# Another order for the attention row: scores, then attention products, then the transposes of both heads

## The chip, the cores and the metric

The kernel runs on one core of a Trainium2 chip. The metric is the device time of one execution in microseconds (us). Before the change three runs took 401.72, 405.03 and 405.11 us, median 405.03 us.

## The reference: what is computed

Inputs are q, k and v (4 batches, 8 heads, 768 positions, 64 numbers per head). For each block of 32 keys a summary key (the maximum over the block) and a summary value (the mean) are made. Each query sees the keys less than 16 positions away and all 24 summaries:

```
scores_l = scale * q @ k^T            (masked to |i - j| < 16)
scores_s = scale * q @ k_sum^T + log(32)
a        = softmax(concat(scores_l, scores_s))
x        = a @ concat(v, v_sum)       -> heads side by side: 4 x 768 x 512
h        = relu(x @ w_in)             -> 4 x 768 x 1024
gate     = sigmoid(conv of h over 3 positions)
out      = (h * gate) @ w_out         -> 4 x 768 x 512
```

All of it is float32. The two large products are made from float32r parts, three products each (high x high, high x low, low x high).

## The kernel before

**Tiling.** The sequence of each batch is cut into two halves, which gives 8 chunks of 384 positions (`NCHUNK`). In each chunk the 8 heads are taken as 4 pairs. A pair is one *row* of attention work; there are 32 rows. The first product of a chunk (x @ w_in, `f1`, line 404) is cut into 8 *units* of 128 hidden features; a unit is 12 matmuls into one PSUM bank. The second product (`f2`, line 473) is cut into tiles of 128 positions; its matmuls are dealt out over the units, 6, 9 or 12 of them after each first product.

**A row.** A row has three sorts of matmul on TensorE (PE in the profile): the scores of a pair (`qk`, line 260, tile `pq`, 24 passes), the transposes of the softmax of each head (`tr`, line 308, tile `pt`, three per head) and the attention products (`av`, line 329, tile `xp`, 24 passes). They belong to different pairs: in the step with number j the scores are those of pair j/2, the transposes those of the pair before, the attention products those of the pair before that. Around them, VectorE (DVE) subtracts the maximum (line 278), ScalarE (ACT) does six exponentials (288) and a small sum (296), VectorE the reciprocal (297), GpSimd (POOL) scales (300). ACT copies a transposed head out of PSUM (315, `aT`). The attention product leaves PSUM as a high part (ACT, 349, `xh`) and a low part (DVE, 350, `xl`), and these are the input of the first product of the next chunk.

**The gate chain of a unit.** After `f1`: relu (ACT 422), middle tap (ACT 425, or DVE 427 in chunks 3, 5, 6 and 7), two taps (DVE 434), tanh (ACT 451), gate multiply (DVE 452, the last reader of the unit's PSUM bank), high part `ghi` (ACT 455), low part `glo` (POOL 456). `gates(1)` issues the multiply of a unit two units later.

**What sets the order.** In chunks 0 and 1 a scheduler orders all engines. From chunk 2 on (`ORDERED`) PE runs in the order in which `unit` writes it, and only the other engines are ordered by the scheduler. A step j falls in unit u of chunk c by j = 8(c+1) + 3 + u, so even steps, which hold the row, fall in odd units. In such a unit the order on PE is: transposes of the first head, attention products, scores, transposes of the second head, first product, second product. Odd steps (even units) hold loads, and for the rows of an even chunk one small transpose `pv` (line 234), which turns the summary values; its result `vm` is copied by ACT (236).

**PSUM.** There are eight banks: two for `pq` (tag s), one for all `pt` (tag t), one that `xp` and `pv` share (tag x), three for the first product (tag f1), one for the second (tag f2). Buffers of a tag are dealt out in turn, and a matmul that takes a buffer waits until the last reader of its former owner is done.

Of the kernel before, what the change touches and what calls it, by code (L numbers as in the profile page):

```python
# [7 lines left out]
F32 = mybir.dt.float32  # L8
# [8 lines left out]
P = 128  # L17
# [8 lines left out]
NP = H // 2  # L26
# [19 lines left out]
ORDERED = 2  # L46
# [4 lines left out]
def attention_ffn(ctx, tc, qT, kT, vT, v4, w_in, cwT, w_out, mask8, ident_in, out):  # L51
# [3 lines left out]
    ps = ctx.enter_context(tc.tile_pool(name="ps", bufs=1, space=bass.MemoryType.PSUM))  # L55
# [19 lines left out]
    def warm(where, after=None):  # L75
        def go():
            for i in range(WARM.get(where, 0)):
                nc.tensor.matmul(pw, idle[:, :P], idle, start=True, stop=True)  # L78

        if after is None:  # L80
            go()
        else:
            with tc.issue_after(after):
                go()
# [28 lines left out]
    def split_in(fc, t):  # L113
        weights(t, flat(win_hi, fc), flat(win_lo, fc), f"i{fc}")
# [6 lines left out]
    def split_out(fc, t):  # L121
        weights(t, wout_hi[:, fc, :], wout_lo[:, fc, :], f"o{fc}")
# [14 lines left out]
    for tag in ("xh", "xl"):  # L137
        t = sp.tile([P, 2, KL], F32, tag=tag, name=f"k_{tag}", bufs=2)
        spare += [t[:, 0, :], t[:, 1, :]]

    def ins(x):
        return getattr(x, "ins", x)
# [7 lines left out]
    def load_k(c, p):  # L150
        b, hf = divmod(c, 2)
        i = c * NP + p
        st = state[(c, p)] = {}
        if i == NP - 1:
            kw = sp.tile([P, 1024], F32, tag="stage", name=f"kw{i}", bufs=2)
            st["kw"] = kw[:, : CB * NK].rearrange("p (b k) -> p b k", b=CB)
        else:
            st["kw"] = sp.tile([P, CB, NK], F32, tag="kw", name=f"kw{i}", bufs=3)
        if hf == 0:
            if c == 0:  # L160
                k = spare[p]
            else:
                k = sp.tile([P, KL], F32, tag="kT", name=f"kT{i}", bufs=2)
            nc.sync.dma_start(k, kT[b, p, :, :KL])
            st["k"] = k
        if c:
            first = kT[b, p, :, hf * CH : hf * CH + WK]
            nc.sync.dma_start(st["kw"][:, :, :WK], window(first, 1, [SP, P], WK))

    def load_vt(c, p):  # L170
        b, hf = divmod(c, 2)
        i = c * NP + p
        if hf:
            return
        if b == 0:
            v = raw_b[:, 2 + p, :S].bitcast(F32)
        else:
            v = sp.tile([P, 1024], F32, tag="stage", name=f"vt{i}", bufs=2)[:, :S]
        nc.sync.dma_start(v, vT[b, p])
        state[(c, p)]["vt"] = v  # L180

    def load_q(c, p):
        b, hf = divmod(c, 2)
        q = sp.tile([P, CH], F32, tag="q", name=f"q{c}_{p}", bufs=4)
        nc.sync.dma_start(q, qT[b, p, :, hf * CH : (hf + 1) * CH])
        state[(c, p)]["q"] = q

    def load_v(c, p):
        b, hf = divmod(c, 2)
        i = c * NP + p  # L190
        va = sp.tile([P, CB, P], F32, tag="va", name=f"va{i}", bufs=4)
        first = v4[b, p, hf * CH : hf * CH + WK, :]
        nc.sync.dma_start(va[:WK, :, :], window(first, P, [P, WK], P))
        state[(c, p)]["va"] = va

    def load_vm(c, p):
        vm = state[("vm", c // 2, p)]
        nc.sync.dma_start(
            state[(c, p)]["va"][WK:NK, :, :], vm.unsqueeze(1).to_broadcast([NB, CB, P])
        )  # L200
# [20 lines left out]
    def vmean_pair(c, p):  # L221

        b, hf = divmod(c, 2)
        if hf:
            return
        st = state[(c, p)]
        vs = sp.tile([P, NB], F32, tag="vs", name=f"vs{c}_{p}", bufs=2)
        nc.vector.tensor_reduce(
            vs, st["vt"].rearrange("p (n t) -> p n t", t=BLK), AX.X, ALU.add
        )  # L230
        pv = ps.tile(
            [P, 512], F32, tag="x" if c else "f1", name=f"pv{c}_{p}", bufs=1 if c else 3
        )
        nc.tensor.transpose(pv[:NB, :P], vs, ident)  # L234
        vm = cp.tile([NB, P], F32, tag=f"vm{p}", name=f"vm{c}_{p}")
        nc.scalar.activation(vm, pv[:NB, :P], AF.Copy, scale=1.0 / BLK)
        if c == 0:
            nc.gpsimd.tensor_copy(
                st["va"][WK:NK, :, :], vm.unsqueeze(1).to_broadcast([NB, CB, P])
            )  # L240
        state[("vm", b, p)] = vm
# [6 lines left out]
    def qk(c, p):  # L248


        st = state[(c, p)]
        n = c * NP + p
        pq = [
            ps.tile([P, 512], F32, tag="s", name=f"pq{n}_{h}", bufs=2) for h in range(2)
        ]
        for blk in range(CB):
            i, half = divmod(blk, 2)
            for h in range(2):
                r = slice(h * QB, (h + 1) * QB)
                last = nc.tensor.matmul(  # L260
                    pq[h][half * QB : (half + 1) * QB, i * NK : (i + 1) * NK],
                    st["q"][r, blk * QB : (blk + 1) * QB],
                    st["kw"][r, blk, :],
                    start=True,
                    stop=True,
                )
        if c == 0:
            warm(f"pq{p}", ins(last))
        softmax(n, c % 2, pq)
# [33 lines left out]

    def tr(j):
        a = state.pop(("a", j))
        pt = ps.tile([P, 512], F32, tag="t", name=f"pt{j}")
        for i in range(3):
            last = nc.tensor.transpose(pt[:NK, i * P : (i + 1) * P], a[:, i, :], ident)  # L308
        if j < 2 * NP:
            warm("tr", ins(last))  # L310
        aT = sp.tile([P, 3 * P], F32, tag="aT", name=f"aT{j}", bufs=3)
        if j < 2 * NP and j % 2:
            nc.vector.tensor_copy(aT[:NK, :], pt[:NK, : 3 * P])
        else:
            nc.scalar.copy(aT[:NK, :], pt[:NK, : 3 * P])  # L315
        state[("aT", j)] = aT
# [42 lines left out]
    def slot(j):  # L359

        if j % 2 == 0:
            n = j // 2 + 2
            if NP <= n < npair:
                load_k(*divmod(n, NP))
                load_vt(*divmod(n, NP))
            if NP <= j // 2 < npair:
                load_vm(*divmod(j // 2, NP))
            if j // 2 < npair:
                qk(*divmod(j // 2, NP))
        else:  # L370
            n = (j + 1) // 2
            if NP <= n + 1 < npair:
                load_q(*divmod(n + 1, NP))
            if n < npair:
                c, p = divmod(n, NP)
                if c:
                    vmean_pair(c, p)
                    load_v(c, p)
                prep_pair(c, p)

    def slot_t(j):
        if 0 <= j - DEPTH < NGROUP:
            tr(j - DEPTH)

    def slot_av(j):
        n = j - DEPTH - 2
        if n % 2 == 0 and 0 <= n < NGROUP:
            av(n // 2)
# [166 lines left out]
    def rooms():  # L555
        gated["hi"] = cp.tile([P, NFC, S], F32R, name="ghi", tag="big_a")
        gated["lo"] = cp.tile([P, NFC, S], F32R, name="glo", tag="big_b")
# [12 lines left out]
    def unit(c, u, pieces, together):  # L570


        j = 8 * (c + 1) + 1 + DEPTH + u
        last = c == NCHUNK - 1
        if together and j % 2 == 0:


            slot_t(j)
            slot_av(j)
        slot(j)  # L580
        if together and j % 2 == 0:
            slot_t(j + 1)
        elif together and c == ORDERED and u == 0:
            slot_t(j)
        if c == 0 and u < 2:
            for fc in (4 + 2 * u, 5 + 2 * u):
                split_in(fc, raws[fc])
        if c == 0 and u == 2:
            rooms()
        gates(1)  # L590
        early = c == 0 and u < EARLY_IN
        if not early:
            f1(c, u, [0, 1])
        if not together:
            slot_t(j)
        done = f1(c, u, [3] if early else [2, 3])
        if c == 0:
            warm("unit", ins(done))
        gate_conv(c, u)
        pending.append((c, u))  # L600
        assert len(pending) <= 2
        if not together:
            slot_av(j)
        for x in pieces[u]:
            f2(*x)
        if last:
            gates(0)
        at = NFC * c + u
        for fc in range(NFC):
            if OUT_AT[fc] == at:  # L610
                split_out(fc, raws["o", fc])
        for fc in range(NFC):
            if OUT_AT[fc] == at + 1:
                raws["o", fc] = load_out(fc)
# [71 lines left out]
```

## Time and profile before

| what | value |
|---|---|
| three runs | 401.72, 405.03, 405.11 us |
| profiled execution | 405.19 us, span 403.3 us |
| PE busy | 387.8 us (96%) |
| DVE, ACT, POOL busy | 262.9, 255.8, 150.3 us |
| chain that ended last | PE 85%, ACT 5%, DVE 3%, DMA 3%, POOL 2% |
| mean granted TensorE clock | 0.987 |

The 1.9 us between the profiled execution and its span lie around the span. A timeline row gives the start of an instruction, its length, engine, line, result and operands; matmuls overlap, so the time that one takes from the next is read from start to start. Chunks 0 and 1 end at about 130 us; the rows that the change touches stand from 134 to 330 us.

### The profile page before, as it was taken

Reading aid. Unit: us, or ns where it says so; the run is one execution under the profiler, and the core shown is the slowest. Engines: PE = TensorE matmul, PEld = TensorE weight load, DVE = VectorE, ACT = ScalarE, POOL = GpSimd, SP = SyncE. Lnnn points to the kernel's source line nnn. Section 1 sums busy time; section 2 is a strip of 40 time slices with the busy share of each in tenths; the row PEclk is TensorE's granted clock in tenths of the full one; section 3 lists DMA queues with packets and bytes.
Section 4 is the critical chain, followed back from the end, with each engine's and each line's share of the span. In section 5 each row is a group of like instructions: output and inputs, shape, how many; then the busy total and the mean of one; then the engine's idle time right before and its main releaser. Section 6 shows DMA issues by size and latency. Waiting matters only on the chain.

```text
span 403.3 us, 8835 instructions
## 1 busy us (share of the span) xinstructions
PE 387.8 (96%) x3173; PEld 322.2 (80%) x3173; DVE 262.9 (65%) x777; ACT 255.8 (63%) x806; POOL 150.3 (37%) x179
## 2 busy tenths in 40 slices
PE   8989879999989999999999999999999999999996
PEld 3546558787768888888888888888888888999884
DVE  4889969998976665667765466466565655556200
ACT  3575699998876787766666778666666653343211
POOL 2316565377764234332333333332422242222200
PEclk9999799999899999999999999999999999999999
DMA  8999783666896784546233343334220000000011
GB/s 293 337 367 191 203 212 119 210 199 194 237 205 188 229 261 127 150 148 199 68 101 112 79 114 113 101 98 120 67 63 28 28 2 26 26 28 27 28 52 52
DMA packets 60715, 54.47 MB, mean 135 GB/s; under 512 B 24640, under 2 KB 51328, under 8 KB 60672
## 3 DMA queue, kind: packets, MB, share of 16 engines
q1 hardware_dynamic: 56928, 47.19, 41.2%
q10 hardware_dynamic: 3744, 6.73, 4.5%
q8 instruction: 25, 0.41, 0.5%
q14 instruction: 18, 0.15, 0.1%
HBM read 45.55 MB, written 6.29 MB: 129 GB/s over the span
## 4 chain that ended last, share of the span: by engine, by line
PE 85%; ACT 5%; DVE 3%; DMA 3%; POOL 2%; issue 1%; SPq 0%; DVEq 0%; POOLq 0%
PE f L473 33%; PE f L404 32%; PE pq L260 7%; PE xp L329 5%; PE pt L308 5%; PE pw L78 3%; ACT a L288 2%; DMA va<-v 2%; DMA k_xh<-kT 1%; POOL wout_lo L128 1%; DVE a L300 1%; POOL glo L456 0%; ACT wu_o L97 0%; ACT t L425 0%; PE pv L234 0%
## 5 line engine op out<-in xcount | busy, mean ns | idle before, releaser
L456 POOL TENSOR_TENSOR glo<-t,ghi 128x383 fp32r<-128x383 f32 (+1 forms) x64 | 66.3, 1037 | 138.3 <-ACT ghi L455 125.9
L404 PE MATMUL f<-xh,win_hi 128*128 128x384 f32 (+1 forms) x256 | 92.5, 361 | 0.9 <-ACT win_hi L127 0.9
L434 DVE SCALAR_TENSOR_TENSOR t<-f,cw,t 128x382 f32<-128x382 f32 (+3 forms) x128 | 78.8, 615 | 19.2 <-ACT t L425 16.6
L404 PE MATMUL f<-xl,win_hi 128*128 128x384 f32 (+1 forms) x256 | 87.9, 344 | 0.0
L404 PE MATMUL f<-xh,win_lo 128*128 128x384 f32 (+1 forms) x256 | 87.2, 341 | 0.0
L288 ACT ACTIVATE a<-a,nm 128x120 f32<-128x120 f32 x192 | 73.4, 384 | 12.3 <-DVE nm L278 12.1
L473 PE MATMUL f<-wout_lo,ghi 128*128 128x512 f32 x192 | 75.7, 394 | 1.6 <-POOL wout_lo L128 1.6
L473 PE MATMUL f<-wout_hi,ghi 128*128 128x512 f32 x192 | 76.4, 398 | 0.0
L473 PE MATMUL f<-wout_hi,glo 128*128 128x512 f32 x192 | 75.0, 391 | 0.0
L300 POOL TENSOR_TENSOR a<-a,sm 128x360 f32<-128x360 f32 x56 | 45.7, 837 | 45.6 <-ACT f L422 28.1
L451 ACT ACTIVATE t<-t 128x383 f32<-128x383 f32 (+1 forms) x64 | 33.6, 526 | 40.3 <-DVE t L434 39.6
L452 DVE SCALAR_TENSOR_TENSOR t<-t,f 128x383 f32<-128x383 f32 (+1 forms) x64 | 35.2, 552 | 29.6 <-ACT t L451 29.6
L404 PEld LDWEIGHTS f<-xh,win_hi 128*128 128x128 f32 x256 | 49.3, 192 | 5.1 <-ACT win_hi L127 1.2
L404 PEld LDWEIGHTS f<-xl,win_hi 128*128 128x128 f32 x256 | 49.2, 192 | 1.4 <-issue 0.3
L404 PEld LDWEIGHTS f<-xh,win_lo 128*128 128x128 f32 x256 | 48.9, 191 | 0.2
L278 DVE CUSTOM_DVE_ANT_0 a<-pq,mask 128x120 f32<-128x120 f32 x192 | 42.7, 275 | 1.5 <-PE pq L260 1.3
L473 PEld LDWEIGHTS f<-wout_lo,ghi 128*128 128x128 f32 x192 | 36.1, 188 | 7.9 <-POOL wout_lo L128 2.2
L473 PEld LDWEIGHTS f<-wout_hi,glo 128*128 128x128 f32 x192 | 36.1, 188 | 7.7
L473 PEld LDWEIGHTS f<-wout_hi,ghi 128*128 128x128 f32 x192 | 36.2, 188 | 7.0 <-issue 0.5
L315 ACT COPY aT<-pt 120x384 f32<-120x384 f32 x60 | 28.2, 470 | 20.7 <-PE pt L308 20.7
L422 ACT ACTIVATE f<-f 128x384 f32<-128x384 f32 (+1 forms) x64 | 30.4, 475 | 15.8 <-PE f L404 15.6
L308 PE MATMUL pt<-ident,a 128*120 128x128 f32 x192 | 33.7, 283 | 5.1 <-ACT aT L315 3.1
(59 smaller groups left out, 508.8 us busy)
## 6 DMA issues: line engine op xcount, KB each, us to landing
va<-v SPq DMA_DIRECT2D x32, 288.0 KB, 4.2
kw<-kT SPq DMA_DIRECT2D x28, 288.0 KB, 6.4
q<-qT SPq DMA_DIRECT2D x32, 192.0 KB, 4.5
out_dram<-ob ACTq DMA_DIRECT2D x24, 256.0 KB, 2.0
kT<-kT SPq DMA_DIRECT2D x12, 392.0 KB, 3.9
vt<-vT SPq DMA_DIRECT2D x12, 384.0 KB, 4.3
wo<-w_out SPq DMA_DIRECT2D x8, 512.0 KB, 5.3
raw_a<-w_in SPq DMA_DIRECT2D x6, 512.0 KB, 11.5
```

What stands on the lines that cost most here:

```text
L260: last = nc.tensor.matmul(pq[h][half * QB : (half + 1) * QB, i * NK : (i + 1) * NK], st["q"][r, blk * QB : (blk + 1) * QB], st["kw"][r, bl ...
L278: nc.vector.tensor_tensor_reduce(a[:, i, :], pq[h][:, i * NK : (i + 1) * NK], mask[:, hf, i, :], -0.125, 3.0e38, ALU.add, ALU.min, nm[:, h ...
L288: nc.scalar.activation(a[:, i, :], a[:, i, :], AF.Exp, bias=nm[:, h, i : i + 1], scale=-1.0, accum_out=sm[:, h, i : i + 1],)
L300: (nc.gpsimd if n >= NP else nc.vector).tensor_tensor(a, a, sm[:, h, :].unsqueeze(2).to_broadcast([P, 3, NK]), ALU.mult)
L308: last = nc.tensor.transpose(pt[:NK, i * P : (i + 1) * P], a[:, i, :], ident)
L404: last = nc.tensor.matmul(ph[:, :n], w[:, fc, cc, :], x[:, cc, :n], start=(cc == 0 and m == 0), stop=(cc == NCC - 1 and m == 2),)
L422: nc.scalar.activation(h[:, :n], h[:, :n], AF.Relu)
L434: nc.vector.scalar_tensor_tensor(t[:, i0:i1], h[:, hf + k - 1 + i0 : hf + k - 1 + i1], cw[:, fc, k : k + 1], t[:, i0:i1], ALU.mult, ALU.add,)
L451: nc.scalar.activation(t, t, AF.Tanh, scale=0.5)
L452: nc.vector.scalar_tensor_tensor(t, t, 1.0, h[:, hf : hf + ng], ALU.add, ALU.mult)
L456: nc.gpsimd.tensor_tensor(gated["lo"][:, fc, d0 : d0 + ng], t, hi.bitcast(F32), ALU.subtract)
L473: nc.tensor.matmul(po, gx[:, fc, ss], w[:, fc, :], start=(fc == 0 and m == 0), stop=(fc == NFC - 1 and m == 2),)
```

## The change

From chunk 2 on the row is written in another order: scores, attention products, transposes of the first head, transposes of the second head, then the first product as before. The transposes of the second head no longer use the bank of tag t but take a buffer of the three of tag f1.

```
     def tr(j):
         a = state.pop(("a", j))
-        pt = ps.tile([P, 512], F32, tag="t", name=f"pt{j}")
+
+        own = j % 2 == 0 or j <= 2 * NP * (ORDERED + 1) + 1
+        pt = ps.tile(
+            [P, 512], F32, tag="t" if own else "f1", name=f"pt{j}", bufs=1 if own else 3
+        )
...
         j = 8 * (c + 1) + 1 + DEPTH + u
         last = c == NCHUNK - 1
         if together and j % 2 == 0:
-
-
+            slot(j)
+            slot_av(j)
             slot_t(j)
-            slot_av(j)
-        slot(j)
-        if together and j % 2 == 0:
             slot_t(j + 1)
-        elif together and c == ORDERED and u == 0:
-            slot_t(j)
+        else:
+            slot(j)
+            if together and c == ORDERED and u == 0:
+                slot_t(j)
```

There are 18 such rows (units 1, 3, 5, 7 of chunks 2 to 5, units 1 and 3 of chunk 6), and in unit 5 of chunk 6 a row without scores. The lines behind `tr` stand 4 lines further down in the changed kernel (308 becomes 312, 422 becomes 426, and so on).

The order on PE in unit 5 of chunk 4 before (pt: transposed head, xp: attention products, pq: scores, f_4_5: first product of the unit):

```order
L308 MATMUL pt_3206<-ident,a_0_3106 120x128 x3
L329 MATMUL xp_3212<-aT_3066,va_2888 64x64
...
L260 MATMUL pq_0_3234<-kw_2948,q_0_3026 64x120
...
L308 MATMUL pt_3268<-ident,a_1_3113 120x128 x3
L404 MATMUL f_4_5_3278<-xh_2393,win_hi 128x384
```

and now:

```order
L260 MATMUL pq_0_3213<-kw_2923,q_0_3026 64x120
...
L333 MATMUL xp_3247<-aT_3122,va_2888 64x64
...
L312 MATMUL pt_3262<-ident,a_0_3085 120x128 x3
L312 MATMUL pt_3268<-ident,a_1_3092 120x128 x3
L408 MATMUL f_4_5_3278<-xh_2424,win_hi 128x384
```

The scores come first and the six transposes stand together ahead of the first product.

The order on ACT from the relu of unit 2 to the relu of unit 3 in chunk 4 before (f_4_2, f_4_3: first products, by relu; t_1, t_2: gate tiles, by tap and tanh; a_0, a_1: the exponentials of the row's two heads; ob: a finished tile of the output):

```order
L422 ACTIVATE f_4_2_3035<-f_4_2_3035 128x384
L455 CAST ghi<-t_1_3013 128x383
L425 ACTIVATE t_2_3049<-f_4_2_3035,cw 128x383
L482 ACTIVATE ob_2_3059<-f_1_2_2913 128x512
L315 COPY aT_3066<-pt_3062 120x384
L483 DMA out_dram<-ob_2_3059 128x512
L349 CAST xh_2942<-xp_3068 128x384
L451 ACTIVATE t_2_3049<-t_2_3049 128x383
L315 COPY aT_3128<-pt_3124 120x384
L288 ACTIVATE a_0_3106,sm_3105<-a_0_3106,nm_3104 128x120 x3
L288 ACTIVATE a_1_3113,sm_3105<-a_1_3113,nm_3104 128x120 x3
L422 ACTIVATE f_4_3_3134<-f_4_3_3134 128x384
```

and now:

```order
L459 CAST ghi<-t_1_3013 128x383
L426 ACTIVATE f_4_2_3035<-f_4_2_3035 128x384
L429 ACTIVATE t_2_3049<-f_4_2_3035,cw 128x383
...
L455 ACTIVATE t_2_3049<-t_2_3049 128x383
L288 ACTIVATE a_0_3085,sm_3084<-a_0_3085,nm_3083 128x120 x3
L288 ACTIVATE a_1_3092,sm_3084<-a_1_3092,nm_3083 128x120 x3
L353 CAST xh_2977<-xp_3103 128x384
L296 ACTIVATE sm_3084<-sm_3084 128x6
L319 COPY aT_3122<-pt_3118 120x384
L319 COPY aT_3128<-pt_3124 120x384
L426 ACTIVATE f_4_3_3134<-f_4_3_3134 128x384
```

The high part `xh` and both copies `aT` have moved from ahead of the exponentials to behind them, ahead of the relu of unit 3; and the cast of unit 1 now stands ahead of the relu of unit 2.

The order on DVE around the row of unit 5 of chunk 4 before (t_4: gate tile of unit 4; nm, a: the maximum step of the row):

```order
L452 SCALAR_TENSOR_TENSOR t_4_3193<-t_4_3193,f_4_4_3179 128x383
L350 TENSOR_TENSOR xl_2943<-xp_3212,xh_2942 128x384
L278 ISA a_0_3250,nm_3248<-pq_0_3234,mask 128x120
...
L278 ISA nm_3248 128x1
L297 RECIPROCAL sm_3249<-sm_3249 128x6
```

and now:

```order
L456 SCALAR_TENSOR_TENSOR t_4_3193<-t_4_3193,f_4_4_3179 128x383
L278 ISA a_0_3229,nm_3227<-pq_0_3213,mask 128x120
...
L278 ISA nm_3227 128x1
L354 TENSOR_TENSOR xl_2978<-xp_3247,xh_2977 128x384
L297 RECIPROCAL sm_3228<-sm_3228 128x6
```

The low part `xl` has moved behind the six maximum steps.

## Rows read from the trace of the kernel before

**Rows 1.** Windows: stretch, length, busy us (instructions) by engine, granted clock, DMA share, GB/s.

```profile
130.00:173.00 43.00, 43.00 (x387) 37.95 (x387) 27.62 (x87) 32.20 (x102) 14.91 (x20) 1.00 0.65 195
```

**Rows 2.** Page, part 4: the chain that ended last, by engine.

```profile
PE 85%; ACT 5%; DVE 3%; DMA 3%; POOL 2%; issue 1%; SPq 0%; DVEq 0%; POOLq 0%
```

**Rows 3.** Timeline, PE, the row in unit 3 of chunk 4.

```profile
230.60 0.39 PE L473 MATMUL f<-wout_hi,glo 128*128 128x512 f32 x1
230.83 0.49 PE L308 MATMUL pt<-ident,a 128*120 128x128 f32 x3
231.25 0.92 PE L329 MATMUL xp<-aT,va 120*64 120x64 f32 x24
232.10 0.84 PE L260 MATMUL pq<-kw,q 64*64 64x120 f32 x24
232.88 0.55 PE L308 MATMUL pt<-ident,a 128*120 128x128 f32 x3
233.18 0.42 PE L404 MATMUL f<-xh,win_hi 128*128 128x384 f32 x1
```

**Rows 4.** Timeline, PE, other neighbours of these matmuls: chunk 1, and the row without scores.

```profile
82.53 0.49 PE L308 MATMUL pt<-ident,a 128*120 128x128 f32 x3
82.77 0.42 PE L404 MATMUL f<-xh,win_hi 128*128 128x386 f32 x1
...
107.25 0.40 PE L473 MATMUL f<-wout_lo,ghi 128*128 128x512 f32 x1
107.49 0.39 PE L473 MATMUL f<-wout_hi,glo 128*128 128x512 f32 x1
107.81 0.62 PE L260 MATMUL pq<-kw,q 64*64 64x120 f32 x6
108.36 0.45 PE L329 MATMUL xp<-aT,va 120*64 120x64 f32 x6
...
328.63 0.92 PE L329 MATMUL xp<-aT,va 120*64 120x64 f32 x24
329.48 0.54 PE L308 MATMUL pt<-ident,a 128*120 128x128 f32 x3
329.78 0.42 PE L404 MATMUL f<-xh,win_hi 128*128 128x384 f32 x1
```

**Rows 5.** Timeline, ACT, units 2 to 5 of chunk 4.

```profile
229.64 0.47 ACT L422 ACTIVATE f<-f 128x384 f32<-128x384 f32 x1 [0.41 <-PE f L404]
230.03 0.50 ACT L455 CAST ghi<-t 128x383 fp32r<-128x383 f32 x1
...
233.83 0.40 ACT L288 ACTIVATE a<-a,nm 128x120 f32<-128x120 f32 x1
...
236.12 0.47 ACT L422 ACTIVATE f<-f 128x384 f32<-128x384 f32 x1
...
243.10 0.48 ACT L349 CAST xh<-xp 128x384 fp32r<-128x384 f32 x1
...
244.42 0.39 ACT L288 ACTIVATE a<-a,nm 128x120 f32<-128x120 f32 x1 [0.15 <-DVE nm L278]
...
246.71 0.46 ACT L315 COPY aT<-pt 120x384 f32<-120x384 f32 x1
...
247.18 0.47 ACT L422 ACTIVATE f<-f 128x384 f32<-128x384 f32 x1
```

**Rows 6.** Timeline, DVE, units 3 to 5 of chunk 4.

```profile
234.42 0.55 DVE L452 SCALAR_TENSOR_TENSOR t<-t,f 128x383 f32<-128x383 f32 x1
...
243.17 0.55 DVE L452 SCALAR_TENSOR_TENSOR t<-t,f 128x383 f32<-128x383 f32 x1 [0.64 <-ACT t L451]
243.64 0.55 DVE L350 TENSOR_TENSOR xl<-xp,xh 128x384 fp32r<-128x384 f32 x1
```

**Rows 7.** Timeline, PE, the small transposes after units 3 and 5 of chunk 4.

```profile
237.44 0.27 PE L234 MATMUL pv<-ident,vs 128*24 128x128 f32 x1
...
247.62 0.27 PE L234 MATMUL pv<-ident,vs 128*24 128x128 f32 x1
```

## The prediction

> **What bounds the kernel now.** I read three views, in this order. The windows show that TensorE never pauses where the change acts: in the stretch from 130 to 173 us it is busy 43.00 of 43.00 us at a granted clock of 1.00, while ACT is busy 32.20 us and DVE 27.62 us [rows 1]; the stretches up to 344 us read alike. The chain that ended last is 85% PE [rows 2]. So in this region a microsecond counts if TensorE's own sequence becomes shorter or longer, or if TensorE is made to wait where it does not wait now. Work on the other engines counts only through such a wait. The third view is the timeline: a row of attention work on PE [rows 3], the same matmuls beside other neighbours [rows 4], then ACT, DVE and the small transposes behind that row [rows 5 to 7].
>
> **TensorE's own sequence.** From start to start a row costs now: three transposes 0.42 us (230.83 to 231.25), attention products 0.85 (to 232.10), scores 0.78 (to 232.88), three transposes 0.30 (to 233.18), together 2.35 us [rows 3]. The new order needs four prices that this row does not show.
> - From the second product into the scores: the start that follows a second product comes 0.24 us later as a rule (107.25 to 107.49) and 0.32 later where scores follow (to 107.81), so 0.08 to 0.10 us [rows 4].
> - From scores into attention products: 107.81 and 108.36 show them as neighbours, but the row is split there and gives no price [rows 4]. The nearest are today's neighbours: the 0.78 of the scores contains leaving them for another shape, the 0.85 of the products entering from another shape [rows 3]. I take both unchanged.
> - From attention products into transposes: 328.63 to 329.48 is 0.85, the price of today, and the three transposes behind them take 0.30 up to the first product, also today's [rows 3, 4].
> - Three more transposes in the same run: three take 0.24 where the first product follows (82.53 to 82.77), and that product then pays some 0.09 itself, so 0.33 us [rows 3, 4].
>
> The sum is 0.09 + 0.78 + 0.85 + 0.30 + 0.33 = 2.35 us. Before, the row changes the shape on the array three times (transposes to products, products to scores, scores to transposes), and now also three times; transposes and the large products follow each other for nothing. Over 18 rows I put this at 0, with ends of 0.05 us per row either way: -0.9 to +0.9 us.
>
> **Waits taken away.** The second transposes no longer wait for ACT's copy of the first ones. Today that copy is hidden: the second ones start 1.6 us after the first have been issued (231.25 to 232.88) and a copy takes 0.46 [rows 3, 5], and with PE busy all the time there is no wait to remove [rows 1]. Worth 0.
>
> **Waits added: the bank of the first product.** Three buffers are dealt in turn to two first products and one transposed head per two units. So the transposes always meet the same bank, and each first product takes over the bank of the product two units earlier, not three. Behind it everything on PE is queued. The last reader of that bank is the gate multiply: that of unit 2 ends at 234.42 + 0.55 = 234.97 us, and the first product of unit 4 follows the small transpose of 237.44 [rows 6, 7]. That leaves 2.5 us; the wait costs nothing as long as the gates are not later by more than that. The bank of the transposed head was emptied a whole row earlier.
>
> The Trainium skill, "Perfetto Trace Analysis", section "Optimizing Tensor Performance", says that independent groups should rotate through different PSUM banks, so that emptying one overlaps the matmuls of the next. By that rule the second head's own bank would be a gain and the first product's loss of one a cost; the rows above give each of them 0, because both evacuations are already covered, so by rows and rule alike only the one bank that `xp` and `pv` share is left to decide.
>
> **Waits added: ACT's order, and the small transpose.** Here I expect the cost. `pv` shares its bank with the attention products, so it starts only when ACT has made `xh` and DVE `xl`. Both stood ahead of the exponentials and the maximum steps; both now stand behind them. From the start of the six exponentials to the end of `xl` it now takes: exponentials 2.29 us (233.83 to 236.12), `xh` 0.48, `xl` 0.55, and two handovers of some 0.04: 3.4 us [rows 5, 6]. So much behind the exponentials `pv` can start, and PE waits there until it can.
>
> When do the exponentials of unit 5 start? Scores start at 230.83 + 0.09 now instead of 232.10 [rows 3], 1.2 us earlier, which would help. But ACT's order eats it. The relu of unit 3 used to follow the exponentials at once, at 236.12; now `xh`, the small sum and two copies stand between. The pair copy and sum takes 0.47 (246.71 to 247.18), `xh` some 0.4 in sequence and the second copy about as much: 1.2 us [rows 5]. In unit 1 the same happens with one copy and the sum between already, so some 0.8 us; and there the cast of unit 1, which waits for a gate multiply that is itself 0.8 us later, has moved ahead of the relu of unit 2 (229.64 and 230.03 change places [rows 5]). That relu, its taps and its tanh become over a microsecond later, so the exponentials of unit 3 start at about the 233.83 of today in spite of the earlier scores, and the relu of unit 3 comes 1.2 us later. From there to the exponentials of unit 5 (244.42) relu, taps, tanh, next relu, taps, tanh, multiply and cast each start on the end of the one before; `xl` no longer stands ahead of the maximum steps (243.64), which gives back 0.2 us at most, since the cast after the multiply of 243.17 must still come first [rows 5, 6]. The exponentials start at about 245.4, `xl` ends at 248.8, and `pv` was due at 247.62 [rows 7]: a wait of 1.2 us. If all of the earlier scores arrived, the exponentials could start right behind the cast that follows the multiply of 243.17, at about 244.2, `xl` would end at 247.6 and the wait would be 0. Between 0 and 1.2 I take 1.0, near the upper end, because the chain of units 1 to 3 speaks for it.
>
> How often? There are eight `pv` after chunk 1, four in chunks 2 and 3, four in chunks 4 and 5. Unit 5 carries only six matmuls of the second product, the other odd units nine or twelve at 0.23 us each, so `pv` comes 0.7 or 1.4 us later behind those rows. Behind unit 3 it is due at 237.44, with `xl` done at 233.83 + 3.4 = 237.23: no wait [rows 5, 7]. So two places, unit 5 of chunks 2 and 4: 2.0 us. PE has no slack in which to win it back. With waits of 1.2 at these two and 0.7 at all the other six it would be 6.6, the upper end.
>
> **Other engines and queues.** On SP the load of `kw` now goes out ahead of that of `va`, on POOL the copy into `kw` ahead of a low part; both serve a row more than 10 us later, so 0. The transposes of the first head stand 2 us later than before while their scaling on POOL stands where it stood: 0. If that cover went, the transposes would hold up the first product directly.
>
> **Sum.** The profiled execution took 405.19 us, 0.16 above the median. 405.19 + 0 + 2.0 = 407.2, against the median 407.0.
>
> **Rivals.**
> 1. Forecast: two waits ahead of `pv`, 407.0. Chance 0.60.
> 2. Nothing: the earlier scores bring the exponentials forward by as much as the moved copies cost, `xl` ends before `pv` is due. For it: ACT and DVE have a quarter or more of the time free [rows 1]. 405.0. Chance 0.22.
> 3. The first product's two banks decide. If the moved copies add up over the units instead of once per row, and the gates are 3.0 us late, the multiply is 0.5 us too late at each of the 18 rows; this costs 9 us: 414. It decides from 2.5 us of lateness on. Against it: the even units end in pauses of ACT that take up lateness. Chance 0.09.
> 4. Cheaper changes of shape: if entering the scores from the second product, or six transposes in a run, saved one change of some 0.15 us (0.42 beside 0.24 for three transposes [rows 3, 4]) per row, 18 rows give 2.7 us: 402.3. Chance 0.09.
>
> That the change would not do what it says is excluded by the order on PE shown above.
>
> **Numbers.** About 1% (4.05 us) is what a measurement of this kernel can tell from no change. The range runs from 403.7 (the lowest run before plus 2.0 us) to 409.5 (405.0 plus waits of 1.2 us at the two places and of 0.7 at three other `pv`). Over 1% slower: rival 3 and the upper end of the forecast, 0.11. Over 1% faster: part of rival 4 and run scatter, 0.03. Within 1%: 0.86.
>
> **What would show it.** A row of 2.35 us from the end of one second product to the first product shows the price of PE's sequence. `pv` behind unit 5 in chunks 2 and 4 should wait about 1 us for DVE's `xl`, the other six not. The relu of odd units should come about 1 us later behind its first product, and the gate multiply should still end over a microsecond before the first product that takes its bank. PE waiting at the first products, or a row clearly under 2.3 us, would prove me wrong.

## Result and profile after

The changed kernel takes 406.59 us (median, 403.76 to 408.79) beside 404.94 us of the kernel before, so the medians are 1.65 us apart. The ratio, estimated from all of these runs, is 1.0057, 95% interval 1.0032 to 1.0082, which is some 2.3 us. The ratios in this document leave out two slow runs, one of "bank part alone" (413.83 us) and one of "products first, casts ahead" (408.68 us). The forecast was 407.0 us, with a loss of 2.0 us.

The first 130 us carry most of the scatter between runs. The order on TensorE is the same there in every kernel of this document (up to the first product of chunk 2), and yet that stretch took 126 to 131 us in the profiles. So I also compare what lies behind it: from the first product of chunk 2 to the end of the span. That is 403.26 - 129.84 = 273.42 us before; after, it is 404.16 - 128.29 = 275.87, so 2.45 us more. The rows of after, PE at that start and in unit 3 of chunk 4 (to compare with [rows 3]):

```profile
128.29 0.42 PE L408 MATMUL f<-xh,win_hi 128*128 128x384 f32 x1
...
229.13 0.39 PE L477 MATMUL f<-wout_hi,glo 128*128 128x512 f32 x1
229.45 0.84 PE L260 MATMUL pq<-kw,q 64*64 64x120 f32 x24
230.22 0.92 PE L333 MATMUL xp<-aT,va 120*64 120x64 f32 x24
231.07 0.87 PE L312 MATMUL pt<-ident,a 128*120 128x128 f32 x6
231.70 0.42 PE L408 MATMUL f<-xh,win_hi 128*128 128x384 f32 x1
...
236.68 0.28 PE L234 MATMUL pv<-ident,vs 128*24 128x128 f32 x1 [0.56 <-DVE xl L354]
236.72 0.42 PE L408 MATMUL f<-xh,win_hi 128*128 128x384 f32 x1
...
243.32 0.43 PE L408 MATMUL f<-xh,win_hi 128*128 128x384 f32 x1
...
248.09 0.28 PE L234 MATMUL pv<-ident,vs 128*24 128x128 f32 x1 [1.04 <-DVE xl L354]
248.12 0.42 PE L408 MATMUL f<-xh,win_hi 128*128 128x384 f32 x1
```

TensorE's own row costs what it did: 2.25 us from 229.45 to 231.70, and with some 0.1 us of entering the scores 2.35 us. What is new are two waits of `pv`, behind units 3 and 5 of chunk 4. First product to first product the units with them take 5.02 us (231.70 to 236.72) and 4.80 (243.32 to 248.12); before, the same units took 4.29 and 3.59 (first products at 233.18, 237.47, 244.06 and 247.65). That is 0.73 + 1.21 = 1.94 us. PE's waits from 129 us to the end (engine, what waits, whom for: us in all, times, longest), the windows of chunks 2 and 4 (columns as in [rows 1]), and the chain of waits by engine:

```profile
PE pv L234 <- DVE xl L354: 1.6, 2, 1.0
PE f L477 <- ACT ob L486: 0.2, 1, 0.2
```

```profile
130.00:173.00 43.00, 43.00 (x387) 37.55 (x386) 27.46 (x88) 30.61 (x101) 15.33 (x20) 1.00 0.63 185
...
217.00:260.00 43.00, 41.40 (x376) 35.70 (x375) 22.04 (x82) 30.85 (x100) 14.86 (x20) 1.00 0.35 96
```

```profile
PE 69%; ACT 12%; DVE 7%; DMA 5%; issue 3%; SPq 2%; POOL 2%; ACTq 0%; DVEq 0%
```

PE is busy throughout chunk 2; 1.94 of the 2.45 us are lost at the two waits in chunk 4. The chain that ended last was 85% PE [rows 2] and is 69% PE now, with ACT at 12% instead of 5 and DVE at 7% instead of 3. Of the other 0.5 us, 0.35 stand behind the first product of chunk 7 (59.52 us to the end, before 59.17), where the second product waits 0.2 us for `ob`; what makes that wait stays open here. ACT and DVE in chunk 4 (to compare with [rows 5, 6]):

```profile
229.98 0.51 ACT L459 CAST ghi<-t 128x383 fp32r<-128x383 f32 x1 [0.62 <-DVE t L456]
230.40 0.47 ACT L426 ACTIVATE f<-f 128x384 f32<-128x384 f32 x1
...
233.31 0.38 ACT L288 ACTIVATE a<-a,nm 128x120 f32<-128x120 f32 x1
...
235.58 0.46 ACT L353 CAST xh<-xp 128x384 fp32r<-128x384 f32 x1
...
236.04 0.83 ACT L319 COPY aT<-pt 120x384 f32<-120x384 f32 x2
236.78 0.48 ACT L426 ACTIVATE f<-f 128x384 f32<-128x384 f32 x1
...
244.70 0.39 ACT L288 ACTIVATE a<-a,nm 128x120 f32<-128x120 f32 x1
...
246.99 0.46 ACT L353 CAST xh<-xp 128x384 fp32r<-128x384 f32 x1
```

```profile
236.07 0.56 DVE L354 TENSOR_TENSOR xl<-xp,xh 128x384 fp32r<-128x384 f32 x1 [1.55 <-ACT xh L353]
...
240.79 0.55 DVE L456 SCALAR_TENSOR_TENSOR t<-t,f 128x383 f32<-128x383 f32 x1 [0.59 <-ACT t L455]
...
247.47 0.56 DVE L354 TENSOR_TENSOR xl<-xp,xh 128x384 fp32r<-128x384 f32 x1 [2.01 <-ACT xh L353]
```

Measured from its own first product, not on the clock of the trace, ACT is late: the relu of unit 3 starts 236.78 - 231.70 = 5.08 us behind it, before 236.12 - 233.18 = 2.94 [rows 3, 5]. Most of that lateness is not made in this row. It grows over the rows of chunk 3, as a table of relu start minus start of the unit's first product shows (worked out from the traces of four kernels; the last two are experiments below):

| chunk, unit | before | after | casts behind | casts ahead |
|---|---|---|---|---|
| 2, 6 | 2.38 | 2.38 | 2.39 | 2.37 |
| 3, 0 | 2.39 | 2.75 | 2.39 | 2.75 |
| 3, 2 | 2.53 | 3.15 | 2.80 | 2.40 |
| 3, 4 | 2.32 | 3.59 | 2.32 | 2.83 |
| 3, 6 | 2.51 | 4.00 | 2.73 | 2.31 |
| 4, 0 | 2.29 | 3.64 | 2.29 | 2.37 |
| 4, 2 | 2.29 | 4.52 | 2.29 | 3.07 |
| 4, 3 | 2.94 | 5.08 | 3.40 | 3.35 |

Some 2.3 us is the unit's own matmuls: there ACT waits for PE. Above that, ACT is behind. By unit 2 of chunk 4 it is 2.23 us later than before, built up over six rows, so 0.4 us per row on average but not evenly (at unit 0 of chunk 4 it falls back), until PE has to wait for it. In unit 3 of chunk 4 that begins, by an estimate, at some 4.35 us: the 5.08 less the 0.73 that PE lost there.

### The profile page after: what moved, and what is told of

It reads as the page before. It is cut to its first block, busy times and chain, and to the rows that moved or that the text cites. A ratio compares the mean times of both kernels' runs of the same rounds, so it can differ in the third digit from the quotient of the medians.

```text
span 404.2 us, 8845 instructions
## 1 busy us (share of the span) xinstructions
PE 385.8 (95%) x3164; PEld 320.4 (79%) x3173; DVE 260.6 (64%) x777; ACT 252.4 (62%) x806; POOL 150.5 (37%) x179
## 4 chain that ended last, share of the span: by engine, by line
PE 69%; ACT 12%; DVE 7%; DMA 5%; issue 3%; SPq 2%; POOL 2%; ACTq 0%; DVEq 0%
PE f L408 27%; PE f L477 27%; PE pq L260 5%; PE xp L333 4%; ACT a L288 4%; PE pt L312 4%; DVE t L438 3%; PE pw L78 2%; DMA wo<-w_out 1%; DMA k_xh<-kT 1%; ACT f L426 1%; ACT t L455 1%; ACT t L429 1%; ACT aT L319 1%; DMA va<-v 1%
## 5 line engine op out<-in xcount | busy, mean ns | idle before, releaser
L300 POOL TENSOR_TENSOR a<-a,sm 128x360 f32<-128x360 f32 x56 | 45.8, 839 | 62.8 <-ACT aT L319 36.4
L408 PEld LDWEIGHTS f<-xh,win_hi 128*128 128x128 f32 x256 | 49.5, 193 | 4.7 <-issue 1.2
L408 PEld LDWEIGHTS f<-xl,win_hi 128*128 128x128 f32 x256 | 49.5, 193 | 1.4 <-issue 0.3
L459 ACT CAST ghi<-t 128x383 fp32r<-128x383 f32 (+1 forms) x64 | 32.6, 510 | 17.6 <-DVE t L456 16.4
L260 PEld LDWEIGHTS pq<-kw,q 64*64 64x64 f32 x768 | 23.4, 132 | 18.4 <-issue 12.9
L354 DVE TENSOR_TENSOR xl<-xp,xh 128x384 fp32r<-128x384 f32 x32 | 17.8, 555 | 30.2 <-ACT xh L353 29.9
```

Source lines behind the costliest of these rows:

```text
L260: last = nc.tensor.matmul(pq[h][half * QB : (half + 1) * QB, i * NK : (i + 1) * NK], st["q"][r, blk * QB : (blk + 1) * QB], st["kw"][r, bl ...
L300: (nc.gpsimd if n >= NP else nc.vector).tensor_tensor(a, a, sm[:, h, :].unsqueeze(2).to_broadcast([P, 3, NK]), ALU.mult)
L354: nc.vector.tensor_tensor(xl[:, p, o : o + CH], xp[:, :CH], xh[:, p, o : o + CH].bitcast(F32), ALU.subtract,)
L408: last = nc.tensor.matmul(ph[:, :n], w[:, fc, cc, :], x[:, cc, :n], start=(cc == 0 and m == 0), stop=(cc == NCC - 1 and m == 2),)
L459: nc.scalar.copy(hi, t)
```

## Experiments

Two rounds. In the first, theory 1 is the prediction's (`pv` waits in the bank it shares, because `xh` and `xl` stand behind the exponentials), theory 2 that ACT's order as a whole makes the gate chain late and `pv` is only where it shows first, theory 3 the banks or the price of TensorE's row. "Behind 130 us" is the time from the first product of chunk 2 to the end of the span, in the profiled execution, against 273.42 us before.

| kernel | ratio to before, 95% interval | behind 130 us | PE's waits there (view of waits) |
|---|---|---|---|
| after | 1.0057 (1.0032 to 1.0082) | +2.45 | `pv` 1.6, `ob` 0.2 |
| pv in another bank | 1.0039 (1.0007 to 1.0072) | +2.35 | `ob` 1.6 |
| bank part alone | 0.9998 (0.9971 to 1.0025) | +0.01 | none |
| products first | 0.9972 (0.9946 to 0.9999) | +0.02 | none |
| softmax written behind | 1.0069 (1.0033 to 1.0106) | +1.96 | `ob` 1.3 |
| casts behind the relu | 1.0030 (0.9997 to 1.0063) | +0.73 | `ob` 0.2 |
| products first, casts ahead | 1.0020 (0.9987 to 1.0052) | +0.04 | none |
| four shape changes | 1.0107 (1.0050 to 1.0165) | +3.02 | `ob` 0.2 |
| one bank for both heads | one run, 493.57 us | +92.0 | copy `aT` 52.3, `sm` 3.2 |

**pv in another bank.**

```
-            [P, 512], F32, tag="x" if c else "f1", name=f"pv{c}_{p}", bufs=1 if c else 3
+            [P, 512], F32, tag="s" if c > 2 else "x" if c else "f1", ... bufs=2 if c > 2 else 1 if c else 3
```

> The changed kernel, except that from chunk 3 on the small transpose pv takes a buffer of the two that the scores use, no longer the bank of the attention products. Theory 1 (the loss is pv waiting for xh and xl in the bank it shares): the wait of pv for DVE's xl (1.6 us in all in chunk 4) is gone, no other wait grows by more than 0.3 us, and the time comes back by 1.6 to 2 us, to a ratio of about 1.000 against the kernel before (1.002 at most). Theory 2 (ACT's later order is the loss, and pv is only where it shows first): the same lateness turns up at the next bank, the single one of the second product, which waits for ob on ACT; the chunk keeps 1 us or more of its loss, ratio 1.003 to 1.005. Theory 3 (the two banks left to the first product, or a dearer row on TensorE): nothing changes, ratio 1.0055.

Theory 1 falls. The waits of `pv` are gone, and the loss is not. PE's waits in that kernel, and the row of the longest:

```profile
PE f L477 <- ACT ob L486: 1.6, 2, 1.4
```

```profile
249.93 0.50 PE L477 MATMUL f<-wout_hi,ghi 128*128 128x512 f32 x1 [1.37 <-ACT ob L486]
```

With `pv` free, PE goes on for 2.35 us (`pv` starts at 246.21, the wait at 249.93 - 1.37 = 248.56) and then meets the next thing that ACT makes, the finished tile `ob` whose bank the second product needs. That unit, unit 6 of chunk 4, loses 1.62 us. The relu of unit 2 of chunk 4 is as late as after (4.50 us).

**The bank part alone.** The order of before, the second head's transposes in a buffer of the first product's.

```
-        pt = ps.tile([P, 512], F32, tag="t", name=f"pt{j}")
+        own = j % 2 == 0 or j <= 2 * NP * (ORDERED + 1) + 1
+        pt = ps.tile([P, 512], F32, tag="t" if own else "f1", ..., bufs=1 if own else 3)
```

> The bank part alone: the order of the kernel before, with the second head's transposes in a buffer of the first product's three. Theories 1 and 2 (the loss comes from the order in which ACT and DVE now work): ratio 1.000 within 0.002, TensorE without waits in chunks 2 to 5, the second head's transposes start as they did. Theory 3, in its form of the banks (the first product has two banks instead of three and waits for the gate multiply): the loss is all here, ratio 1.005 or more, with waits of the first product for DVE's multiply.

Nothing: 273.43 us, ratio 0.9998. Two banks left to the first product cost nothing, and the second head's own bank brings nothing in that order.

**Products first.** The order av, qk, tr, tr.

```
-            slot(j)
             slot_av(j)
+            slot(j)
             slot_t(j)
             slot_t(j + 1)
```

> The changed kernel with the attention products ahead of the scores in the row, and nothing else changed; xh then stands ahead of the exponentials on ACT, and xl ahead of the maximum steps on DVE. Theories 1 and 2: pv finds its bank empty, TensorE does not wait in chunks 2 to 5, the time from the first instruction of the row to the first product stays 2.35 us (within 0.1), ratio 1.000 within 0.002. Theory 3 (two banks, or six transposes in a run at a dearer price): the loss stays, ratio 1.005.

The loss is gone. PE does not wait and takes 273.44 us, what it took before, so the two kernels are equal where they differ. The interval just under 1 I put down to the first 130 us (127.5 us in this profile, 129.8 before), where TensorE's order is the same; one profile of each does not show it.

**Softmax written behind the products.** TensorE's order as after; ACT now makes `xh` behind none, one or two exponentials of a row instead of six.

```
...
-            slot(j)
+            held_row = slot(j, hold=True)
             slot_av(j)
+            if held_row:
+                softmax(*held_row)
```

> The changed kernel with TensorE's order untouched, but the softmax of the row is written behind the attention products instead of ahead of them, so that ACT makes xh ahead of all or nearly all exponentials of the row and DVE xl earlier. Theory 1: xl ends about 2 us earlier after the row, pv waits at most 0.2 us, and the ratio is 1.000 to 1.002. Theory 2: the exponentials are later by the length of xh, the gate chain behind them stays as late as in the changed kernel, and the second product waits for ob; ratio 1.003 to 1.005. Theory 3: ratio 1.0055, the same as the changed kernel, as TensorE's row and the banks are the same.

ACT and PE in that kernel, around unit 5 of chunk 4:

```profile
246.99 0.51 ACT L461 CAST ghi<-t 128x383 fp32r<-128x383 f32 x1 [0.62 <-DVE t L458]
247.41 0.39 ACT L290 ACTIVATE a<-a,nm 128x120 f32<-128x120 f32 x1
...
247.80 0.46 ACT L355 CAST xh<-xp 128x384 fp32r<-128x384 f32 x1
```

```profile
248.90 0.28 PE L234 MATMUL pv<-ident,vs 128*24 128x128 f32 x1
...
252.57 0.50 PE L479 MATMUL f<-wout_hi,ghi 128*128 128x512 f32 x1 [1.31 <-ACT ob L488]
```

`xh` is done earlier and `pv` does not wait, yet 1.96 us are lost, 1.55 of them in unit 6 of chunk 4, where the second product waits for `ob`. So the place of `xh` behind all six exponentials is not what costs. The ratio is above what theory 2 expected, but its first 130 us took 131.0. Theory 2 stands; theories 1 and 3 don't.

What in ACT's order is it? Comparing the orders of after and of "products first", the casts stand out: after has the `ghi` of an odd unit ahead of the next unit's relu at eight places: units 0 and 4 of chunk 3, units 0 and 2 of chunks 4 and 5, and units 0 and 4 of chunk 6 (the expectations below say seven and leave out the last). "Products first", like the kernel before, has it so at two of them, unit 0 of chunks 4 and 6. The table agrees: from row to row, the lateness of after above that of before rises by 0.36, 0.65 and 0.88 us up to units 0 and 4 of chunk 3 and unit 2 of chunk 4, where the cast is newly ahead, and changes by -0.14 to 0.26 up to the others. ACT around unit 4 of chunk 3, after, and then with the cast behind:

```profile
194.80 0.53 ACT L455 ACTIVATE t<-t 128x385 f32<-128x385 f32 x1 [1.62 <-DVE t L438]
195.95 0.51 ACT L459 CAST ghi<-t 128x385 fp32r<-128x385 f32 x1 [0.62 <-DVE t L456]
196.37 0.47 ACT L426 ACTIVATE f<-f 128x386 f32<-128x386 f32 x1
```

```profile
196.47 0.53 ACT L456 ACTIVATE t<-t 128x385 f32<-128x385 f32 x1 [1.62 <-DVE t L439]
197.12 0.48 ACT L427 ACTIVATE f<-f 128x386 f32<-128x386 f32 x1
197.62 0.52 ACT L460 CAST ghi<-t 128x385 fp32r<-128x385 f32 x1
```

After, the relu follows the tanh of the unit before by 1.57 us, because the cast between them waits for DVE's multiply. With the cast behind it follows by 0.65, when PE has the unit ready; the cast then finds its multiply done. The Trainium skill, "PSUM — Partial Sum Buffer", section "Engine vs sequencer instructions", calls ScalarE's and VectorE's queues strict FIFO; by that rule one waiting cast holds up all of ACT behind it, and these rows agree: the relu of after starts only behind the cast.

**Casts behind the relu.** After, with only that order fixed.

```
...
-        nc.scalar.copy(hi, t)
+        cast = nc.scalar.copy(hi, t)
+        if c >= ORDERED and fc % 2 and (nxt := divmod(c * NFC + fc + 1, NFC)) in relus:
+            tc.add_manual_dep(ins(cast), ins(relus[nxt]).name, ...)  # order alone, no wait
```

> The changed kernel with TensorE's order and the banks untouched and one order on ACT fixed: from chunk 2 on, the cast ghi of an odd unit stands behind the relu of the next unit, as in the kernel before (in the changed kernel seven casts stand ahead of that relu, so that the relu waits until the gate multiply before it is done). xh and both copies aT stay behind the exponentials. Theory A (these casts make the gate chains of two units follow each other on ACT and DVE, and this is what makes ACT later pair by pair): the relu of unit 2 of chunk 4 starts at most 3 us behind its first product instead of 4.5, no wait of TensorE over 0.3 us from chunk 2 to chunk 5, ratio 1.000 to 1.002. Theory B (it is xh and the two copies in one block behind the exponentials): relu stays 4 to 5 us behind, the waits of pv stay at 1.5 us or more, ratio 1.0055.

**Products first, casts ahead.** The other way about: the kernel that did not lose, with the casts put ahead at the first seven of these places.

```
...
+        if (c, fc) in AHEAD:  # (3, 0), (3, 4), (4, 0), (4, 2), (5, 0), (5, 2), (6, 0)
+            tc.add_manual_dep(ins(relu), ins(casts["last"]).name, ...)
...
-        gates(1)
+        gates(0 if (c, u) in AHEAD else 1)
```

> The row with the attention products first (which did not lose), with the casts of odd units put ahead of the next relu at the seven places where the changed kernel has them; xh stays ahead of the exponentials. Theory A (the casts suffice): the relu of unit 2 of chunk 4 is 4 us or more behind its first product, TensorE waits 1.5 us or more for pv or the second product, ratio 1.004 or more. Theory B, and a theory C (both are needed: the casts and the copies behind the exponentials, as each alone leaves the pauses of ACT that take up lateness): relu at most 3 us behind at unit 2 of chunk 4, no wait over 0.3 us, ratio 1.000 within 0.002 of that of the kernel without the casts.

Both columns stand in the table above. With the casts behind, lateness no longer builds up (2.29 us at unit 2 of chunk 4) and the loss falls from 2.45 to 0.73 us; what is left is 0.3 us in unit 5 of chunk 4 and 0.4 near the end. With the casts ahead but `xh` ahead of the exponentials too, each cast that is newly ahead makes ACT 0.4 to 0.8 us later, and 1.3 where two follow each other (3.66 us at unit 2 of chunk 5), the rows behind it give that back, and PE never waits: 273.46 us. The edit also moves a tanh behind the relu in units 2 and 6 of chunk 3; the lateness is given back where no tanh moved, too (2.94 us at unit 4 of chunk 4, "products first" 2.67).

So theory C in its main point: the casts alone do not lose the 2 us, the row's new order alone loses 0.73, and both together lose 2.45; most of it hangs on the two meeting. What in the row's order must meet the casts is read from ACT's orders, not tested by itself. ACT around unit 2 of chunk 4, casts ahead:

```profile
227.18 0.51 ACT L469 CAST ghi<-t 128x383 fp32r<-128x383 f32 x1 [0.62 <-DVE t L466]
227.60 0.47 ACT L428 ACTIVATE f<-f 128x384 f32<-128x384 f32 x1
...
229.65 0.48 ACT L353 CAST xh<-xp 128x384 fp32r<-128x384 f32 x1 [0.41 <-ACT ob L496]
...
230.95 0.40 ACT L288 ACTIVATE a<-a,nm 128x120 f32<-128x120 f32 x1
```

The cast waits ahead of the relu as in after (229.98 and 230.40 there), but `xh` is made in a pause of ACT ahead of the exponentials, where after makes it at 235.58, behind them and with no pause before it. In the kernels that lose nothing `xh` stands ahead of all six exponentials in each of the 18 rows; in "softmax written behind" it has moved up only to the first exponentials, behind the pause, and 1.96 us are lost. So, by this reading, the cast costs ACT a pause, and with `xh` out of the pauses ACT has too little left to get it back. Of the copies this is not shown: in "products first" and in "casts ahead" both stand behind the exponentials in 10 of the 18 rows, and nothing is lost. Nor is TensorE's order separated from the place of `xh`: no kernel here has the scores first and `xh` in a pause.

Of theory A the first half is borne out by "casts behind", with a ratio just above what it expected; that the casts suffice is refuted. The ratio of "casts ahead" is 0.005 above that of "products first", more than theory C allowed, but behind 130 us the two are the same within 0.02 us.

**Four shape changes.** Scores, transposes, products, transposes, with `pv` in a buffer of the scores.

```
             slot(j)
-            slot_av(j)
             slot_t(j)
+            slot_av(j)
             slot_t(j + 1)
```

> The changed kernel with the attention products between the two heads' transposes (scores, transposes, products, transposes), and pv in a buffer of the scores. TensorE's row then changes the shape on the array four times instead of three. If a change costs some 0.15 us, as the prediction worked out from three transposes, the row takes 2.50 us instead of 2.35, 18 rows are 2.7 us, and the ratio is 1.006 to 1.010, depending on how much of ACT's lateness is taken up by the longer row. If changes of shape are free, the row stays at 2.35 us and the ratio at 1.004 or below.

PE in unit 3 of chunk 4 of that kernel:

```profile
228.47 0.39 PE L477 MATMUL f<-wout_hi,glo 128*128 128x512 f32 x1
228.78 0.85 PE L260 MATMUL pq<-kw,q 64*64 64x120 f32 x24
229.56 0.54 PE L312 MATMUL pt<-ident,a 128*120 128x128 f32 x3
230.03 0.92 PE L333 MATMUL xp<-aT,va 120*64 120x64 f32 x24
230.88 0.54 PE L312 MATMUL pt<-ident,a 128*120 128x128 f32 x3
231.18 0.42 PE L408 MATMUL f<-xh,win_hi 128*128 128x384 f32 x1
```

From 228.78 to 231.18 is 2.40 us instead of 2.25: one more change, 0.15 us. Eighteen of them are 2.7 of the 3.02 us. The casts stand ahead here at the same eight places and `xh` behind the exponentials, and yet PE has no wait before the 0.2 us near the end: the relu of unit 2 of chunk 4 is 3.20 us behind instead of 4.52, which fits a longer row on PE taking up much of ACT's lateness. The Trainium skill, "TensorEngine Tiling (Array Packing)", section "Key Properties", says that changing the tiling mode drains TensorE, without a price. This row gives one for one more change of shape; that draining is what takes the time, no run here shows. The ratio lies a little above the expected range, with an interval that takes it in.

**One bank for both heads.** After's order, the bank part undone.

```
-        own = j % 2 == 0 or j <= 2 * NP * (ORDERED + 1) + 1
-        pt = ps.tile([P, 512], F32, tag="t" if own else "f1", ..., bufs=1 if own else 3)
+        pt = ps.tile([P, 512], F32, tag="t", name=f"pt{j}")
```

> The changed kernel's order with the second head's transposes back in the one bank of tag t: the bank part of the change undone. The second transposes must wait until ACT has copied the first ones out, and that copy stands behind six exponentials, xh and the sum on ACT: some 3 us from the end of the first transposes to the copy's end. All theories: 18 waits of the transposes for ACT's copy of 2.5 to 3.3 us each, 45 to 60 us in all, about 455 us. If the copy were as well hidden as in the kernel before, the time would be that of the changed kernel.

PE's waits, and windows of chunks 2 and 3 (columns as in [rows 1]):

```profile
PE pt L309 <- ACT aT L316: 52.3, 18, 3.5
PE pt L309 <- ACT sm L296: 3.2, 1, 3.2
```

```profile
130.00:173.00 43.00, 33.68 (x273) 29.25 (x272) 19.71 (x64) 22.75 (x73) 11.14 (x15) 0.88 0.43 126
173.00:216.00 43.00, 34.19 (x275) 29.84 (x274) 22.01 (x68) 21.83 (x71) 11.47 (x15) 0.88 0.47 129
```

The waits are what was expected, 55.5 us. The time is not: 92.0 us are lost, 36.5 more than TensorE waits. The granted clock is 0.88 here, where every other kernel has 1.00. Behind a wait of 2.81 us the first product's matmuls follow each other at 0.32 us, where after has 0.17:

```profile
150.69 0.64 PE L309 MATMUL pt<-ident,a 128*120 128x128 f32 x3 [2.81 <-ACT aT L316]
...
151.45 0.52 PE L405 MATMUL f<-xl,win_hi 128*128 128x384 f32 x1
151.77 0.52 PE L405 MATMUL f<-xh,win_lo 128*128 128x384 f32 x1
```

So the two parts of the change belong together: with this order the second head needs its bank.

## Why the prediction was right, and where not

- **The row's price.** Right: 2.35 us from the end of the second product, for three changes of shape as before. A fourth change cost the 0.15 us that the prediction took from the two sorts of transposes.
- **The copy wait taken away is worth 0; the first product's two banks cost 0.** Right, by "the bank part alone". The multiply of unit 3 ends at 241.34, 1.98 us ahead of the first product of unit 5 (243.32); it was 2.5 us at unit 4 before.
- **The cost at `pv`.** The size was right: 1.94 us where 2.0 was forecast, at two places. Of the places one was: unit 5 of chunk 4, 1.21 us for the 1.0 forecast. The other was unit 3 of chunk 4 (0.73 us), where the prediction had no wait, instead of unit 5 of chunk 2, which lost nothing. The failed step is "how often": I worked out one row's lateness and let it begin anew in every chunk. It adds up, by 0.4 us per row on average, from the end of chunk 2 through chunk 3. In chunk 2 the row's relu was 0.2 to 0.5 us later, not 1.2.
- **The cause.** Half right. `pv` did wait for `xl`, but the shared bank and the six exponentials ahead of `xh` were not what cost: 2.35 us were lost without the shared bank, and 1.96 with `xh` ahead of at least four of the six. I had named the cast that moved ahead of the relu and the copies that moved behind the exponentials, as reasons for ACT's order eating the earlier scores. Without the casts ahead 0.73 of the 2.45 us are left, and with the casts ahead but the products first 0.04: it takes the casts together with the row's new order. That the copies cost anything is not shown. `pv` is only the first place where the lateness meets PE.
- **The time of the exponentials.** I put those of unit 3 at 233.83, as today, with the earlier scores paid back. Against their first product they start 1.61 us later now (233.31 - 231.70) and started 0.65 later before (233.83 - 233.18): 1.0 us of lateness that the row had inherited.
- **The rivals.** Of rival 3's condition, "the moved copies add up over the units", the adding up came about, though not shown to be the copies'; its price did not, since `pv` and `ob` stop PE before the gate multiply can: 1.98 us of that reserve were left when `pv` waited. Rival 4's cheaper changes did not show. That the result fell into the range owes something to luck: one place less in chunk 2 and one more in chunk 4. The 0.35 us near the end had no term in the prediction.

## What to carry to other kernels

Measure an engine's lateness against the engine that leads it, unit by unit; a difference that grows by 0.4 us per row is invisible as a wait until, some 65 us later here, it is one. When a wait is found, freeing the bank it stands at is no cure if the engine behind it is late: the next bank takes over. Where one engine's order by a scheduler follows another's by hand, compare both orders, and look for an instruction that waits ahead of one that is ready.

## What the runs showed of the hardware

- With TensorE made to wait 2.6 to 3.5 us in every row, its granted clock fell to 0.80 to 0.90 in the windows from 130 to 420 us, so it worked part of the time at the lower of its two levels, 1.2 GHz, with 0.32 us between matmuls of the first product instead of 0.17. With waits of 55.5 us the kernel lost 92.0 us.
- A row with three changes of shape on the array takes 2.25 us from its first matmul to the first product in after and in "products first" (228.61 to 230.86), a row with four 2.40 us: 0.15 us for one change more.
- Profiles of the same order on TensorE differ by 3.7 us in chunk 0 alone, 45.8 to 49.5 us from its first product to that of chunk 1. The granted clock goes with it, 1.00 in the first 80 us of the short ones and 0.94 to 0.96 in the long ones; which of the two is the cause, no run shows.
